# Delta-rule attention and a matmul MLP on one core: diagonal blocks of 32 solved whole from the third pair on, other norms and other unpacking in the first

## The chip, the cores and the metric

The kernel runs on one core of a Trainium2 chip. The metric is device time in microseconds (us), median of several executions. The engines are named as in the profile: PE is TensorE (PEld its weight load), DVE is VectorE, ACT is ScalarE, POOL is GpSimd, SP issues most of the DMAs.

## The reference, cut to what matters

```python
q, k, v: (4, 8, 768, 48)        beta: (4, 8, 768)
k_n = k / (norm(k) + 1e-06)
state = 0                                            # (4, 8, 48, 48)
for t in range(768):
    y[t]  = q[t] @ state
    v_old = k_n[t] @ state
    state = state + beta[t] * outer(k_n[t], v[t] - v_old)
x = y, heads side by side                            # (3072, 384)
h = x @ w_in                                         # w_in (384, 2048)
g = where(h >= 1, h, where(h <= -1, 0, (h + 1) ** 2 / 4))
return g @ w_out                                     # w_out (2048, 384)
```

The recurrence is computed in chunks of 64 steps. Within a chunk the corrected values U solve a unit lower triangular system of 64 by 64 per batch and head, built from the gram matrix of the keys, its diagonal (the squared norms) and beta; so each chunk needs the inverse of such a matrix, 32 of them at a time.

## The kernel before, in words

**Chunks and pairs.** There are 12 chunks g of 64 steps. Two chunks make a pair G, six pairs in all. For a chunk, `gram` (L138) forms K K^T and the masked K Q^T of all 32 heads, in four pieces; K K^T goes to `GG` by ACT (L147), K Q^T goes by two masked DVE multiplications (L151) into the tile `W`, which held the loaded keys and queries. The blocks of 32 on the diagonal are then transposed by DVE into "lanes" (`lanes`, L188 to L217): each of the 128 partitions holds one 32 by 32 block of the pair, so 128 small triangular systems are solved side by side along the free axis.

**The solve.** `solve` (L219) inverts the two diagonal blocks of 16 of each lane with 15 steps of two DVE instructions: a product of a column with a row (L225) and a subtraction (L227), each over 30 to 128 elements. `unlanes` (L230) scales by beta over the squared norm and transposes back (L237, L239). TensorE then joins blocks of 16 to blocks of 32 in `merge16_a` and `merge16_b` (L244, L256: 64 matmuls of 32 by 32 with 16 columns per chunk and step; each is two instructions in the trace), and blocks of 32 to 64 in `merge32_a` and `merge32_b` (L270, L286). With the inverse at hand a chunk goes through `chain_r` (V minus what the state predicts), `chain_u` (U), `chain_y` (the outputs y, which become the MLP's input tile `XB`; six small DMAs on SP per chunk, L353, shift rows) and `chain_d` (the state's update), L301 to L376.

**Norms of V.** `scale_v` (L168) scales V by the norms of its keys, which it works out again from the keys in token order: squares on ACT (L173), a reduction (L176) and five small operations (L161 to L165) on DVE.

**The MLP.** A pair gives 512 tokens. Its MLP is a loop over 16 slices of 128 hidden units, called items here: `up` (L469, nine matmuls with 512 columns), three ACT passes (L579 twice, L597) and a DVE maximum (L605), a rounding to fp32r on ACT (L574) and the remainder on DVE (L575), then `down` (L484, twelve matmuls with 384 columns). `down` of an item is issued two items later; `up` has two buffers, so it waits for the maximum of two items before. During the MLP of pair G the next pair, G+1, is prepared: `plan` (L503) writes by hand at which half item each TensorE block (`pe`) and each piece of DVE and ACT work (`fill`) is put between the MLP's instructions. The MLP of the first pair is cut differently: the first eight items only for its first chunk, eight for both, eight for the second chunk, 24 in all.

**Weights.** The MLP weights arrive as raw 64-bit words and are unpacked into two fp32r parts once (`weight`, L117: one ACT multiplication L122, DVE operations L124, L126, L128, an ACT rounding L132, a DVE subtraction L134, all over 768 elements). `unpack` (L395) hands these out in small steps, some in the opening and the rest in the first pair's items.

**The opening.** Before the first item the first two chunks are loaded and prepared with nothing to hide behind: grams, lanes, solve, merges, then chains, written out one after the other (L418 to L445). `stage` (L413) runs TensorE blocks, then evicts their results, then runs some fill.

## Time and profile before

| what | value |
|---|---|
| time, median of 3 runs | 724.34 us (724.22 to 724.47) |
| the profiled execution's own time | 723.49 us |
| its span, first to last instruction | 721.8 us |
| busy: PE, DVE, ACT, POOL | 650.7, 427.3, 402.1, 31.5 us |
| mean granted TensorE clock | 0.937 of full |
| first `up` of the first pair begins | 75.75 us |
| first `up` of the second pair's MLP begins | 233.69 us |

The profile is of one execution; times in it are counted from its first instruction. A row of a "windows" answer gives, for a stretch from A to B us, its length, the busy time of PE, PEld, DVE, ACT and POOL with their instruction counts, the granted clock, the DMA share and the GB/s moved. A timeline row gives start, length, engine, line, operation, output and inputs, and in brackets the idle time of the engine before it and what ended it; "issue" there is time in which the profile shows nothing that the engine waits for. A row of the groups gives the count, then busy us and mean ns of one.

### The profile page before, as it was taken

How to read it: one execution, taken by the hardware profiler on the slowest of the kernel's cores; microseconds unless marked ns; L12 is line 12 of the kernel's file. 1: busy time of each engine (PE TensorE's matmuls, PEld its weight loads, DVE VectorE, ACT ScalarE, POOL GpSimd, SP SyncE). 2: the span in 40 equal slices, each digit the busy share in tenths (PEclk: the TensorE clock that was granted, in tenths of full speed). 3: DMA queues.
4: the chain of work that ended last, by engine and by line, in shares of the span. 5: the costliest groups of instructions: out<-in, count | busy, mean ns of one | idle time of the engine just before them, and what ended most of it. 6: DMA issues, size and time to landing. Idle time of an engine off the chain costs nothing.

```text
span 721.8 us, 23444 instructions
## 1 busy us (share of the span) xinstructions
PE 650.7 (90%) x10436; PEld 570.0 (79%) x10436; DVE 427.3 (59%) x926; ACT 402.1 (56%) x736; POOL 31.5 (4%) x70
## 2 busy tenths in 40 slices
PE   7048768786899998999999999999999999999996
PEld 7048757565898887888888888888888888898996
DVE  4835999996346884247874347973448862433332
ACT  2017664573565563844664754657555647566663
POOL 1012000000100001000001000001000000000000
PEclk9556886897999999999999999999999999999999
DMA  9950510000017100033100033100142100001001
GB/s 244 416 233 10 157 55 1 0 1 2 11 43 185 27 1 4 3 108 107 45 2 5 5 110 102 44 4 4 29 119 68 45 4 4 13 12 45 1 1 44
DMA packets 18933, 41.72 MB, mean 58 GB/s; under 512 B 3984, under 2 KB 9488, under 8 KB 18832
## 3 DMA queue, kind: packets, MB, share of 16 engines
q1 hardware_dynamic: 17664, 38.81, 18.0%
q8 instruction: 82, 1.34, 0.8%
q10 hardware_dynamic: 912, 1.33, 0.7%
q0 software_dynamic: 256, 0.08, 0.1%
q14 instruction: 19, 0.16, 0.1%
HBM read 33.13 MB, written 4.72 MB: 52 GB/s over the span
## 4 chain that ended last, share of the span: by engine, by line
PE 73%; DVE 10%; ACT 6%; issue 2%; ACTq 0%; DVEq 0%
PE o L484 26%; PE h L469 25%; PE ch L143 4%; PE ch L319 3%; PE ch L339 3%; PE ch L363 2%; PE ch L305 2%; PE ch L248 2%; PE ch L260 2%; DVE wt L134 2%; PE ch L291 2%; PE ch L275 1%; ACT wx L122 1%; DVE s L605 1%; ACT s L579 1%
## 5 line engine op out<-in xcount | busy, mean ns | idle before, releaser
L469 PE MATMUL h<-xb,wt 128*128 128x512 f32 (+1 forms) x936 | 230.9, 391 | 7.9 <-DVE s L605 7.1
L484 PE MATMUL o<-wt,ghi 128*128 128x384 f32 x768 | 206.7, 350 | 0.5 <-issue 0.5
L469 PEld LDWEIGHTS h<-xb,wt 128*128 128x128 f32 x936 | 165.2, 192 | 45.1 <-DVE s L605 9.5
L605 DVE TENSOR_TENSOR s<-h,s 128x512 f32<-128x512 f32 (+1 forms) x104 | 67.2, 646 | 139.4 <-ACT s L597 139.2
L484 PEld LDWEIGHTS o<-wt,ghi 128*128 128x128 f32 x768 | 139.6, 192 | 9.2 <-issue 2.5
L484 PE MATMUL o<-wt,glo 128*128 128x384 f32 x384 | 132.0, 344 | 1.3 <-DVE glo L575 1.3
L579 ACT ACTIVATE s<-h,half 128x512 f32<-128x512 f32 (+1 forms) x104 | 68.1, 655 | 93.3 <-PE h L469 93.1
L575 DVE TENSOR_TENSOR glo<-s,ghi 128x512 fp32r<-128x512 f32 (+1 forms) x104 | 67.1, 645 | 46.5 <-ACT ghi L574 45.6
L574 ACT CAST ghi<-s 128x512 fp32r<-128x512 f32 (+1 forms) x104 | 61.1, 587 | 56.1 <-DVE s L605 49.3
L484 PEld LDWEIGHTS o<-wt,glo 128*128 128x128 f32 x384 | 73.4, 191 | 3.2 <-DVE glo L575 2.9
L579 ACT ACTIVATE s<-s,one 128x512 f32<-128x512 f32 (+1 forms) x104 | 71.9, 692 | 2.2
L597 ACT ACTIVATE s<-s 128x512 f32<-128x512 f32 (+1 forms) x104 | 62.3, 599 | 3.3
L143 PE MATMUL ch<-W 48*64 48x128 f32 x336 | 44.5, 286 | 10.5 <-ACT s L579 5.3
L143 PEld LDWEIGHTS ch<-W 48*64 48x64 f32 x336 | 39.1, 141 | 16.2 <-issue 9.7
L151 DVE TENSOR_TENSOR W<-ch,mask 64x256 f32<-64x256 f32 x84 | 35.5, 422 | 25.2 <-ACT GG L147 24.0
L248 PE MATMUL ch<-XT,GG 32*32 32x16 f32 x1536 | 17.9, 188 | 33.6 <-DVE XT L237 21.2
L248 PEld LDWEIGHTS ch<-XT,GG 32*32 32x32 f32 x1536 | 16.4, 118 | 37.8 <-issue 29.1
L144 PE MATMUL ch<-W 48*64 48x128 f32 x336 | 44.4, 286 | 0.0
L144 PEld LDWEIGHTS ch<-W 48*64 48x64 f32 x336 | 39.1, 141 | 0.0
L122 ACT ACTIVATE wx<-wt 128x768 f32<-128x768 f32 x16 | 14.8, 922 | 29.4 <-DVE wt L134 29.4
L147 ACT COPY GG<-ch 128x256 f32<-128x256 f32 x42 | 15.2, 372 | 27.9 <-PE ch L144 27.9
L374 DVE TENSOR_TENSOR SU<-ch,SU 48x384 f32<-48x384 f32 x40 | 22.2, 555 | 9.2 <-PE ch L363 8.5
(113 smaller groups left out, 732.0 us busy)
## 6 DMA issues: line engine op xcount, KB each, us to landing
wt<-in_w_dram SPq DMA_DIRECT2D x16, 768.0 KB, 14.8
KV<-in_kv_dram SPq DMA_DIRECT2D x24, 384.0 KB, 4.6
W<-in_kqb_dram SPq DMA_DIRECT2D x44, 128.0 KB, 3.4
W<-in_kqa_dram SPq DMA_DIRECT2D x22, 192.0 KB, 3.7
...
W<-in_kqa_dram ACTq DMA_DIRECT2D x2, 192.0 KB, 6.2
```

Of the source, the lines that this page charges most:

```text
L143: nc.tensor.matmul(gp[0:C, p], w_[C:C + D, 0, u, :], w_[C:C + D, 0:2, u, :], start=True, stop=True)
L144: nc.tensor.matmul(gp[C:P, p], w_[0:D, 0, u, :], w_[0:D, 0:3:2, u, :], start=True, stop=True)
L151: nc.vector.tensor_tensor(out=w_[r:r + C, s, us[0]:us[0] + NP], in0=gp[r:r + C, :, 1, :], in1=mask[r:r + C, None, :].broadcast_to([C, NP, ...
L248: nc.tensor.matmul(y[r:r + 32, u], GG[r:r + 32, g, u, 32:64], XT[r:r + 32, g, u, 48:64], start=True, stop=True)
L374: nc.vector.tensor_tensor(out=dst, in0=d_ps[ft:ft + D], in1=dst, op=ALU.add)
L469: nc.tensor.matmul(h[:, cols(bs)], WT[f][:, 0, x, k * P:(k + 1) * P], XB[G][:, y, k, cols(bs)], start=(n == 0), stop=(n == 8))
L484: nc.tensor.matmul(oacc[G, k], (ghi, glo)[x][:, k * P:(k + 1) * P], WT[f][:, 1, y, :], start=(new and n == 0), stop=(left[G, b] == 0 and n ...
L574: nc.scalar.copy(out=ghi[:, c], in_=s[:, c])
L575: nc.vector.tensor_tensor(out=glo[:, c], in0=s[:, c], in1=ghi[:, c], op=ALU.subtract)
L579: nc.scalar.activation(out=out, in_=in_, func=AF.Relu, bias=bias, scale=scale)
L597: nc.scalar.activation(out=s[:, c], in_=s[:, c], func=AF.Square)
L605: nc.vector.tensor_tensor(out=s[:, c], in0=h[:, c], in1=s[:, c], op=ALU.max)
```

## The change

- **From the third pair on** (G of 2 and more) the lanes' blocks of 32 are solved whole: `solve_whole` does 30 steps of two DVE instructions, in place in `A`, over 30 to 240 elements. One scaling over 1024 elements (before: two over 256) and a POOL `affine_select` and `memset` prepare `A`; `unlanes_whole` scales, transposes to `XT` and from there to `GG`. `merge16_a` and `merge16_b` are not issued for these pairs. The steps are spread over items 2.5 to 9.5 of the MLP, `merge32` moves to item 10.5, the chains and the loads move by one item, the second chunk's `chain_d` by three, the grams of the next pair's first chunk by half an item; those of its second chunk stay where they were.
- **V's norms** come from the lanes (one DVE transpose `N`) in all pairs; the squares, reductions and their small operations go.
- **First two pairs** (chunks 0 to 3): K Q^T leaves PSUM by two ACT copies and is masked by two POOL `affine_select` instructions, not by DVE. In the opening those of the second chunk are put off until after the first part of `lanes`.
- **Opening**: all loads on SP, two of the three loads of a `W` tile joined, two weights loaded ahead of K and V; 20 matmuls of 512 columns on zeros (`hold`) between the grams and the merges; `stage` evicts after its fill; in `merge32_a` the copies of `XT` go to DVE; more unpacking here (26 steps of a finer `unpack`, with four buffers, against 7 of the coarser one).
- **First pair's MLP**: four unpacking steps per item (before: two, each of two or three operations); lanes, solve, merges and chains begin earlier, the latter by three items.
- **Last store**: seven of its eight DMAs on SP (before: four).

The diff, cut:

```diff
-            q.dma_start(out=x[0:C, 0], in_=kqb[g, i][:, 0])
-            q.dma_start(out=x[0:C, 2], in_=kqb[g, i][:, 2])
+            q.dma_start(out=x[0:C, 0:3:2], in_=kqb[g, i][:, 0:3:2])
...
-    load_w(1, nc.scalar)
+    load_w(1)
...
+    weight_loads(0, 2)
     load_kv(0)
     load_kv(1)
-    weight_loads(0, FT)
+    weight_loads(2, FT)
...
             nc.scalar.copy(out=GG[:, g % 2, i * NP:(i + 1) * NP], in_=gp[:, :, 0, :])
+            def raw():
+                for r, s in ((0, 1), (C, 2)):
+                    x = w_[r:r + C, s, us[0]:us[0] + NP]
+                    nc.scalar.copy(out=x, in_=gp[r:r + C, :, 1, :])
+                    nc.gpsimd.affine_select(out=x, in_=x, pattern=[[0, NP], [1, C]], base=0, channel_multiplier=-1,
+                                            compare_op=ALU.is_gt, fill=0.0)
+            if g < 4:
+                return raw
...
+        if G >= WHOLE:
+            nc.vector.scalar_tensor_tensor(out=A, in0=A, scalar=-1.0, in1=gm[:, :, None].broadcast_to([P, 32, 32]), op0=ALU.mult, op1=ALU.mult)
+            nc.gpsimd.affine_select(out=A, in_=A, pattern=[[-1, 32], [1, 32]], base=0, channel_multiplier=0,
+                                    compare_op=ALU.is_gt, fill=0.0)
+            nc.gpsimd.memset(A.rearrange("l c t -> l (c t)")[:, 0:1024:33], 1.0)
+            return
...
+    def solve_whole():
+        A = S["A"]
+        for j in range(1, 31):
+            n, m = j, 31 - j
+            pr = sb.tile([P, 240], F32, name="pr", bufs=1)[:, 0:n * m].rearrange("l (c t) -> l c t", t=m)
+            nc.vector.tensor_tensor(out=pr, in0=A[:, 0:n, j:j + 1].broadcast_to([P, n, m]),
+                                    in1=A[:, j:j + 1, j + 1:32].broadcast_to([P, n, m]), op=ALU.mult)
+            nc.vector.tensor_tensor(out=A[:, 0:n, j + 1:32], in0=A[:, 0:n, j + 1:32], in1=pr, op=ALU.add)
+            yield
+    def unlanes_whole():
+        A, gm = S["A"], S["gm"]
+        nc.vector.tensor_tensor(out=A, in0=A, in1=gm[:, None, :].broadcast_to([P, 32, 32]), op=ALU.mult)
+        yield
+        nc.vector.transpose(out=XT[:, :, :, 32:64].rearrange("p g u t -> p t (g u)"), in_=A.rearrange("l c t -> l t c"))
+        yield
+        for g in range(2):
+            nc.vector.transpose(out=GG[:, g, :, 32:64], in_=XT[:, g, :, 32:64])
             yield
...
     def stage(pieces, *fill):
-        finish(products(*pieces))
+        evicts = products(*pieces)
         for gen, m in fill:
             run(gen, m)
+        finish(evicts)
...
+    def hold(n, m):
+        for _ in range(n):
+            nc.tensor.matmul(idle[:, 0:m], SF[:, 0:P], SF[:, 0:m], start=True, stop=True)
+    hold(KEEP, 512)
...
+            so, un = solve_whole(), unlanes_whole()
...
+            for j in range(1, 31):
+                at(fill, G, 2.5 + H / 2, (so, 1))
+                cost += j * (31 - j) + 150
+                H = int(cost / 9461 * 14)
+            for j in range(4):
+                at(fill, G, 9.5 + j // 2 / 2, (un, 1))
+            T = 1
...
+                for j, f in enumerate((merge32_a, merge32_b)):
+                    for g in range(2):
+                        at(pe, G, 10.5 + j + g / 2, lambda f=f, g=g: f(g))
...
-                at(pe, G, T + 14, *both(chain_d, b))
+                late = 0 if G == 0 else 2
+                at(pe, G, T + 14 + late, *both(chain_d, b))
                 at(fill, G, T + 14, (load_w, b + 2))
-                grams(G, T + 14.5, a + 2)
-                grams(G, T + 15.5, b + 2)
+                grams(G, T + 14 + (G == 0) / 2, a + 2)
+                grams(G, T + 14.5 + (G == 0), b + 2)
```

Where the instructions stand, at the three places that the prediction uses. First DVE in the opening, between its start and the norms; `W` are the loaded keys and queries, `ch`, `h` and `o` PSUM tiles of the grams. Before:

```order
L113 MEMSET XT 128x2048
L151 TENSOR_TENSOR W<-ch,mask 64x256 x4
L151 TENSOR_TENSOR W<-h,mask 64x256 x4
L151 TENSOR_TENSOR W<-o_204,mask 64x256 x2
L151 TENSOR_TENSOR W<-o_216,mask 64x256 x2
L151 TENSOR_TENSOR W<-o_228,mask 64x256 x2
L151 TENSOR_TENSOR W<-o_240,mask 64x256 x2
L199 COPY GG<-GG 32x16x32 x4
L201 STREAM_TRANSPOSE A<-GG 128x1024
```

and now:

```order
L115 MEMSET XT 128x2048
L202 COPY GG<-GG 32x16x32 x4
L204 STREAM_TRANSPOSE A<-GG 128x1024
L207 COPY N_281<-A 128x32
L173 TENSOR_SCALAR r_284<-y_283 128x32
```

The sixteen masks are gone from ahead of the copies into lane order. Second, PE in the opening, from the end of the grams to the first chain; `SU` is the state tile, still zero. Before:

```order
L144 MATMUL o_240<-W 64x128
L248 MATMUL ch<-XT,GG 32x16 x128
L260 MATMUL h<-A_396,XT 32x16 x128
L275 MATMUL o_620<-XT,GG 32x32 x32
L291 MATMUL o_661<-GG 32x32 x32
L275 MATMUL o_706<-XT,GG 32x32 x32
L319 MATMUL o_748<-KV,XT 64x48 x16
```

and now:

```order
L147 MATMUL o_247<-W 64x128
L471 MATMUL ch<-SU 128x512 x20
L281 MATMUL ch<-XT,GG 32x16 x64
L281 MATMUL h<-XT,GG 32x16 x64
L293 MATMUL h<-A_437,XT 32x16 x64
L293 MATMUL o_580<-A_437,XT 32x16 x64
L308 MATMUL o_652<-XT,GG 32x32 x32
L308 MATMUL o_696<-XT,GG 32x32 x32
L324 MATMUL o_737<-GG 32x32 x32
L324 MATMUL ch<-GG 32x32 x32
L352 MATMUL ch<-KV,XT 64x48 x16
```

The twenty `hold` matmuls stand ahead of the first merge, and both `merge32_a` blocks now stand ahead of `merge32_b`. Third, DVE in the MLP of the second pair, in one item in the middle of the solve for the third pair (`s`, `h`, `glo` are the MLP's tiles, `pr` a product, `X` and `A` the lanes' blocks). Before:

```order
L605 TENSOR_TENSOR s<-h,s 128x512
L225 TENSOR_TENSOR pr<-X,A_4530 128x110
L227 TENSOR_TENSOR X<-X,pr 128x2x5x11
L225 TENSOR_TENSOR pr<-X,A_4530 128x120
L227 TENSOR_TENSOR X<-X,pr 128x2x6x10
L575 TENSOR_TENSOR glo<-s,ghi 128x512
L225 TENSOR_TENSOR pr<-X,A_4530 128x126
L227 TENSOR_TENSOR X<-X,pr 128x2x7x9
L225 TENSOR_TENSOR pr<-X,A_4530 128x128
L227 TENSOR_TENSOR X<-X,pr 128x2x8x8
```

and now, an item in the middle of the longer solve:

```order
L671 TENSOR_TENSOR s<-h,s 128x512
L247 TENSOR_TENSOR pr<-A 128x220
L249 TENSOR_TENSOR A<-A,pr 128x11x20
L247 TENSOR_TENSOR pr<-A 128x228
L249 TENSOR_TENSOR A<-A,pr 128x12x19
L640 TENSOR_TENSOR glo<-s,ghi 128x512
L247 TENSOR_TENSOR pr<-A 128x234
L249 TENSOR_TENSOR A<-A,pr 128x13x18
L247 TENSOR_TENSOR pr<-A 128x238
L249 TENSOR_TENSOR A<-A,pr 128x14x17
```

As many instructions per item as before, each over about twice the elements, and for seven items in place of four.

More of the change, by code (lines that the diff above doesn't have):

```diff
@@ L168, in scale_v @@
     def scale_v(g):
[L170 to L171 removed]
         for i in range(NT):
[L173 to L183 removed]
+            v, u = KV[g, i][:, 1], g % 2 * NU + i * NV
+            nc.vector.tensor_tensor(out=v, in0=v, in1=S["N"][:, u:u + NV, None].broadcast_to([P, NV, D]), op=ALU.mult)
+            yield
     S = {}
@@ L205, in lanes @@
         r = norms(n)
+        N = S["N"] = sb.tile([P, 32], F32, name="N3")
+        nc.vector.transpose(out=N, in_=n)
         gm = S["gm"] = sb.tile([P, 32], F32, name="gm")
@@ L268, in merge16_b, with merge32_a @@
         return evict
-    def merge32_a(g):
+    def merge32_a(g, first=False):
         y1 = ps.tile([P, NU, 32], F32, **acc())
@@ L282, in evict @@
             for r in (0, C):
-                nc.scalar.copy(out=XT[r:r + 32, g, :, 0:32], in_=XT[r:r + 32, g, :, 32:64])
+                (nc.vector.tensor_copy if first else nc.scalar.copy)(out=XT[r:r + 32, g, :, 0:32], in_=XT[r:r + 32, g, :, 32:64])
         return evict
@@ L424, in delta_rule_moe @@
+    idle = ps.tile([P, 512], F32, **acc())
+    def hold(n, m):
+        for _ in range(n):
+            nc.tensor.matmul(idle[:, 0:m], SF[:, 0:P], SF[:, 0:m], start=True, stop=True)
+    hold(KEEP, 512)
+    run(ln, 2)
+    for x in raws:
+        x()
+    run(ln)
     run(solve())
     run(unlanes())
-    one_ = lambda f, g: [lambda: f(g)]
-    stage(one_(merge16_a, 0), (sv[0], 1))
-    stage(one_(merge16_a, 1), (sv[0], 2))
-    stage(one_(merge16_b, 0), (wu, 1))
-    stage(one_(merge16_b, 1), (sv[0], 9), (sv[1], 1))
@@ L431, in delta_rule_moe @@
-    stage(one_(merge32_a, 0), (wu, 1))
-    stage(one_(merge32_b, 0), (sv[1], 2))
-    stage(one_(merge32_a, 1), (wu, 1))
-    stage(both(chain_u, 0), (sv[1], 9))
-    stage(one_(merge32_b, 1))
-    stage(both(chain_y, 0), (wu, 1))
+    one_ = lambda f, *a: [lambda: f(*a)]
+    stage(one_(merge16_a, 0), (wu, 2))
+    stage(one_(merge16_a, 1), (wu, 2))
+    stage(one_(merge16_b, 0), (sv[0], 2), (wu, 1))
+    stage(one_(merge16_b, 1), (wu, 3))
+    stage(one_(merge32_a, 0, True), (wu, 2))
+    stage(one_(merge32_a, 1, True), (wu, 2))
@@ L437, in delta_rule_moe @@
+    stage(one_(merge32_b, 0), (wu, 2))
+    stage(one_(merge32_b, 1), (sv[1], 2))
+    stage(both(chain_u, 0), (wu, 3))
+    stage(both(chain_y, 0), (wu, 3))
     load_w(2)
@@ L442, in delta_rule_moe @@
             nc.gpsimd.dma_start(out=beta_sb[r + 16 * x:r + 16 * x + 16, 1:NS, :], in_=beta[q:64:4, 2 + x:ntot:2, :])
-    stage(both(chain_r, 1), (wu, 1))
-    stage(both(chain_u, 1), (wu, 1))
+    stage(both(chain_r, 1), (wu, 2))
+    stage(both(chain_u, 1), (wu, 3))
     spare.clear()
@@ L497, in at, with grams @@
         where.setdefault(2 * first[G] + int(round(2 * t)), []).extend(x)
-    def grams(G, t, g):
+    def grams(G, t, g, dt=0.5):
         for j in range(2):
-            at(pe, G, t + j / 2, *[lambda i=2 * j + x: gram(g, i) for x in range(2)])
+            at(pe, G, t + j * dt, *[lambda i=2 * j + x: gram(g, i) for x in range(2)])
     def plan(G):
@@ L526, in plan @@
-            T = 8
+            grams(G, 4, b)
+            at(fill, G, 4, (ln, 1))
+            at(fill, G, 5, (ln, 1))
+            at(fill, G, 5.5, (ln, 1))
+            at(fill, G, 6, (ln, 9))
+            for j in range(8):
+                at(fill, G, 6.5 + j / 2, (so, 2))
+            at(fill, G, 9, (va, 1))
+            at(fill, G, 9.5, (va, 1))
+            at(fill, G, 10.5, (un, 1))
+            at(fill, G, 11, (un, 9))
+            at(fill, G, 13, (vb, 1))
+            at(fill, G, 14, (vb, 1))
@@ L535, in plan @@
-            for j in range(8):
-                at(fill, G, 2.5 + j / 2, (so, 2))
-            at(fill, G, 6, (un, 1))
-            at(fill, G, 6.5, (un, 9))
-            T = 0
-        if G < NS - 1:
-            for j, f in enumerate((merge16_a, merge16_b, merge32_a, merge32_b)):
-                for g in range(2):
-                    at(pe, G, T + 7 + j + g / 2, lambda f=f, g=g: f(g))
+            at(fill, G, 1.5, (ln, 9))
+            cost, H = 0, 0
+            for j in range(1, 31):
+                at(fill, G, 2.5 + H / 2, (so, 1))
+                cost += j * (31 - j) + 150
+                H = int(cost / 9461 * 14)
@@ new lines, in plan @@
+            for j in range(4):
+                at(fill, G, 9.5 + j // 2 / 2, (un, 1))
+            T = 1
+        if G < NS - 1:
+            if G == 0:
+                for j, f in enumerate((merge16_a, merge16_b, merge32_a, merge32_b)):
+                    for g in range(2):
+                        at(pe, G, T + 7 + j + g / 2, lambda f=f, g=g: f(g))
+            else:
+                for j, f in enumerate((merge32_a, merge32_b)):
+                    for g in range(2):
+                        at(pe, G, 10.5 + j + g / 2, lambda f=f, g=g: f(g))
@@ L595, in delta_rule_moe @@
         finish(evicts)
+        run(wu, 1)
         relu(s[:, c], s[:, c], one, -1.0)
```

101 lines of the change are left out of this document (46 added, 55 removed).

## Prediction

> **What bounds the kernel now.** I read the page's 40 slices (18 us each) first, then windows between the starts of items, then timelines of the opening.
>
> ```profile
> PE   7048768786899998999999999999999999999996
> PEclk9556886897999999999999999999999999999999
> ```
>
> ```profile
> 75.75:166.21 90.46, 71.95 (x569) 59.44 (x567) 83.56 (x156) 52.88 (x98) 2.10 (x5) 0.85 0.14 41
> 166.21:239.04 72.83, 63.29 (x1510) 56.58 (x1510) 37.64 (x91) 41.09 (x92) 3.22 (x8) 0.93 0.23 61
> 265.47:283.72 18.25, 16.02 (x559) 13.09 (x555) 9.32 (x19) 6.61 (x13) 1.04 (x2) 0.91 0.02 4
> 373.22:388.24 15.02, 14.45 (x559) 12.22 (x555) 9.21 (x19) 6.61 (x13) 1.04 (x2) 1.00 0.02 5
> 454.84:471.74 16.90, 16.90 (x85) 15.24 (x85) 14.63 (x46) 11.33 (x20) 0.96 (x1) 1.00 0.19 47
> 478.06:492.14 14.08, 14.04 (x559) 11.99 (x555) 9.19 (x19) 6.62 (x13) 1.07 (x2) 1.00 0.02 6
> 581.63:596.53 14.90, 14.58 (x557) 12.24 (x555) 9.19 (x19) 6.61 (x13) 1.04 (x2) 1.00 0.02 4
> ```
>
> Three stages. To 75.75 us nothing hides anything, and the clock is half for most of it. From 75.75 to 166.21 (first pair's MLP up to the transposes that end the solve) DVE is busy 83.56 of 90.46 us: it bounds. From the second pair's MLP on PE bounds: the four items from 454.84 take 16.90, PE busy all of it, 4.225 per item. There, what PE no longer does is time won, as long as DVE (14.63 of the same 16.90) does not become the bound.
>
> **Merges of 16, pairs three to six.** The four windows of two items each that hold them (18.25, 15.02, 14.08, 14.90) last 62.25 together; eight bare items are 33.80. Removed: **-28.4**, waits in them included.
>
> **DVE in those pairs.** Step prices, from the opening's solve:
>
> ```profile
> 26.12 0.19 DVE L225 TENSOR_TENSOR pr<-X,A 128x30 f32<-128x30 f32 x1
> 30.11 0.29 DVE L225 TENSOR_TENSOR pr<-X,A 128x128 f32<-128x128 f32 x1
> 34.85 0.76 DVE L235 TENSOR_TENSOR A<-X,gm 128x256 f32<-128x256 f32 x2
> ```
>
> From 30 to 128 elements an instruction grows by 0.10, so 0.16 us plus 1.0 ns per element. The old solve lasts 26.12 to 34.85 = 8.7 for 30 instructions over 2720 elements, which by that are busy 7.6: a gap of 0.04 behind each. The new one has 60 over 9920 elements (twice the sum of j(31-j)): 60 x 0.20 + 9.9 = 21.9, or 20 if the gap vanishes wherever the MLP's own instructions come between. What stands beside it:
>
> ```profile
> 427.72:435.80 8.08, 8.08 (x122) 6.92 (x118) 5.17 (x11) 4.41 (x9) 0.33 (x1) 1.00 0.18 43
> 444.20:450.63 6.43, 6.43 (x56) 5.57 (x54) 5.08 (x12) 3.58 (x7) 0.00 (x0) 1.00 0.01 3
> 444.20:478.06 33.86, 33.86 (x246) 30.22 (x244) 28.92 (x75) 20.88 (x35) 0.96 (x1) 1.00 0.10 24
> 471.74:478.06 6.32, 6.32 (x87) 5.60 (x86) 5.07 (x12) 3.49 (x6) 0.00 (x0) 1.00 0.01 3
> L605 DVE TENSOR_TENSOR s<-h,s 128x512 f32<-128x512 f32 (+1 forms) x104 | 67.2, 646 | 139.4 <-ACT s L597 139.2
> L374 DVE TENSOR_TENSOR SU<-ch,SU 48x384 f32<-48x384 f32 x40 | 22.2, 555 | 9.2 <-PE ch L363 8.5
> L151 DVE TENSOR_TENSOR W<-ch,mask 64x256 f32<-64x256 f32 x84 | 35.5, 422 | 25.2 <-ACT GG L147 24.0
> 476.81 2.25 DVE L237 STREAM_TRANSPOSE XT<-A 128x1024 f32<-128x1024 f32 x1
> ```
>
> DVE from item 0 to the transposes that merge32 waits for, by item 9.5: 28.92 of items 0 to 6; less the old steps, their two scalings of 0.76 and the transpose begun there at 476.81 (7.6 + 1.5 + 1.3); plus solve 20 to 22, four masks 1.7, chain_d 4 x 0.555 = 2.2, two scalings over 1024 elements 2.4 (by the step's price), transpose 2.2, chain_r's two subtractions some 1.1, and for three more items L605 and the remainder of the same size, 1.3 each: **52.5 to 54.5**. PE in the same stretch, to merge32_a at the end of item 10: 6.43 (item 0 with two grams), 8.08 - 6.43 = 1.65 for chain_d, 6.32 for the item with chain_r, nine others at 4.225: 52.4. A tie. DVE starts about 1 us late, since the grams end first, but an up waits only for the maximum of two items before. What lies over is a wait of PE at merge32_a: 1 to 2 us per pair, **+5** for four (0 to 16). Behind the waiting merge32 stand both chains, so it cannot be made up.
>
> POOL's select over 1024 elements sits between the scaling and the first step. Nearest row:
>
> ```profile
> L101 POOL TENSOR_SCALAR_AFFINE_SELECT mask<-mask 64x64 f32<-64x64 f32 x2 | 0.5, 232 | 0.1
> L216 POOL MEMSET A<- 128x1024 f32 x6 | 5.7, 956 | 162.5 <-DVE A L214 162.5
> ```
>
> Between 0.96 (a memset of that size) and 3.7 (0.232 for 64, scaled). I take 1.5, nearer the memset of equal size, since most of 0.232 looks fixed; it is covered by the MLP's two DVE instructions of 0.65 and a scaling of V that stand between. At 3.7 the solve starts 2 us later, +9 for four pairs; that is in the 16. [...]
>
> **Loads for the second chunk's grams.** These grams stay at items 15.5 and 16; their loads move from item 14 to 15, behind six row DMAs of chain_y, now at 14.5.
>
> ```profile
> 429.33 4.50 SPq L353 DMA_DIRECT2D xb<-X  x6
> 435.16 0.58 SPq L72 DMA_DIRECT2D W<-in_kqa_dram  x1
> W<-in_kqa_dram SPq DMA_DIRECT2D x22, 192.0 KB, 3.7
> ```
>
> The up of the item that starts at 427.72 follows chain_y directly; the row DMAs end 6.1 later, the first tile's last load is issued at 7.4 and lands at 11.1. PE now reaches the gram after up, two grams, down, two grams: 4.2 + 4 x 1.05 = 8.4. It waits 2.7, in three pairs: **+8** (3 to 9). Nothing hides it: PE is in order.
>
> **The opening.**
>
> ```profile
> L97 PE MATMUL o<-wx 128*128 128x128 f32 x28 | 6.1, 414 | 1.1 <-DVE half L104 1.1
> 7.14 0.32 PE L143 MATMUL ch<-W 48*64 48x128 f32 x1
> 10.16 1.28 ACT L108 ACT_TABLE_LOAD   x1 [10.16 <-DMA W<-in_kqa_dram]
> L147 ACT COPY GG<-ch 128x256 f32<-128x256 f32 x42 | 15.2, 372 | 27.9 <-PE ch L144 27.9
> 19.00 1.70 DVE L199 COPY GG<-GG 32x512 f32<-32x512 f32 x4
> 37.97 2.76 PE L248 MATMUL ch<-XT,GG 32*32 32x16 f32 x193 [21.22 <-DVE XT L237]
> 44.71 0.99 PE L248 MATMUL ch<-XT,GG 32*32 32x16 f32 x60 [3.97 <-issue]
> 49.45 0.42 DVE L265 TENSOR_TENSOR XT<-XT,h 128x256 f32<-128x256 f32 x1 [2.03 <-PE h L260]
> 69.70 0.28 DVE L349 TENSOR_TENSOR X<-h,X 128x128 fp32r<-128x128 f32 x1
> 75.75 0.50 PE L469 MATMUL h<-xb,wt 128*128 128x256 f32 x2
> ```
>
> The first gram starts at 7.14, but ACT only at 10.16, after its DMA issues; then the masks hold DVE until 19.00. Now ACT is free and copies as grams end, from about 7.4: twelve copies of 0.37 for the first chunk's grams and four for the second's reach 13.3 (the second chunk's loads no longer share the DMA engines with K and V). Before, DVE's four copies into lane order lasted from 19.00 to 20.70; now the first chunk's two are done by 13.3 and the second's two end 0.85 later, at 14.15, which is 6.55 earlier. The new transpose `N` takes some 0.2 of that; so all down to the merge at 37.97 moves up by about 6.4, to 31.5.
>
> The `hold` matmuls stand before that merge on PE. 28 instructions over 128 columns took 6.1 at the start, 0.22 each; 512 columns in two instructions are 1.74 at that rate, 35 for twenty, and 17 if the clock is twice as fast by then, as the first digit of its row says. From 11.6 (my estimate for the last gram on PE, one or two copies of 0.37 ahead of ACT's last ones) they end at 29, beneath the solve, and cost nothing; at the slow rate they would end at 47.
>
> The merges: in one of them PE lost 3.97 to nothing that the profile shows, while weights still loaded. Starting earlier, more of the merging lies in that time; I add 2. The first result of merge16_b came at 49.45, 11.5 after the first merge; now at 31.5 + 11.5 + 2 = 45. DVE waits for it, then has until chain_y's remainders about 18 to 19 us without a pause: five weights of 3.4 (prices below) and 2 for copies, less what of it came ahead. That is 64; the first up came 6 after the last remainder (69.70, 75.75), so now near 70.3. V's norms, gone, lay beside the merges' waits. **-5.4** (-10 to +10).
>
> **First pair's MLP.**
>
> ```profile
> L134 DVE TENSOR_TENSOR wt<-wx,wt 128x768 fp32r<-128x768 f32 x15 | 14.2, 948 | 0.0
> L128 DVE SCALAR_TENSOR_TENSOR wx<-wt,wx 128x768 int32<-128x768 int32 x14 | 13.3, 952 | 0.0
> L124 DVE TENSOR_SCALAR wx<-wx 128x768 int32<-128x768 int32 x13 | 7.8, 602 | 0.6 <-ACT wx L122 0.6
> ```
>
> A weight costs DVE 0.60 and three times about 0.95 (L126 is of L128's kind): 3.4. Some 3.6 fewer here: -12; sixteen masks x 0.42: -6.7; the solve's transposes come at item 11 instead of 14, three full items' 1.3 off: -4. That leaves 67 to 68 of 90.46; I take 70, for ACT now carries some 8 us in each of the two items with eight copies of 0.37 more. After it PE bounds: before, the 72.83 from 166.21 on held 10 of waits (72.83 - 63.29) and half-clock time (0.93); now it has three full items more in it (12.7) and some 10 less of waits and slow clock: 75.5. **-18** (-10 to -26).
>
> **Small.** A PE idle of 2 to 3 us can lower the clock, as it did in the second pair (0.91 in the first merge window): **+3** (0 to 10). At the end SP issues three DMAs more, of 0.58 each by the row above, while ACT's last copy comes sooner: **+0.5**.
>
> **Sum.** -28.4 + 5 + 8 - 5.4 - 18 + 3 + 0.5 = -35.3. The profiled execution took 723.49 (its span 721.8 and 1.7 around it): 688.2; the median lies 0.85 above it: **689**.
>
> **Rivals.**
>
> (1) *The hold keeps the clock up through merges and chains.*
>
> ```profile
> 60.00:64.00 4.00, 4.00 (x93) 3.91 (x93) 2.21 (x6) 3.83 (x8) 0.00 (x0) 0.50 0.02 4
> 68.00:72.00 4.00, 3.06 (x112) 2.81 (x109) 3.16 (x7) 3.27 (x7) 0.00 (x0) 0.97 0.06 14
> ```
>
> The clock fell in the opening's solve and stayed at 0.50 through merges and chain_u, which kept PE busy 4.00 of 4; it rose at 68. I therefore let it fall again in the merges. If it does not, the chains of the opening run at full speed, -5, and the pairs' +3 goes: 681. [...] Chance 0.17.
>
> (2) *DVE, not PE, bounds pairs three to six*: every gap kept, 3.7 us for the select, the clock falling at each wait: 16 in place of 5 and 10 in place of 3, +18: 707. Chance 0.21.
>
> (3) *The change doesn't do what it says in front*: the hold runs at the slow rate and ends at 47, where the merges would start at 31.5: the opening grows by 10 instead of shrinking by 5.4, 704; with (2) as well, 722. Against it: the clock was full when the grams ended. Chance 0.07, most of it with (2).
>
> (4) *Slower.* In-place steps with a strided column cost more than the old ones: at 0.22 us more on each of 60, DVE needs 13 more per pair, all of it waited for by PE since the two are tied: +53, 742. Slower begins at +35, 0.15 per step. The old steps read a strided column too and show no such cost at 30 or 128 elements. Chance 0.05.
>
> The forecast itself has 0.50, its own range 678 to 700. The range, 669 to 711, takes in (1) and (2), with their errors on the outer side, leaving out (4) and most of (3). Faster by more than 0.2% (1.4 us, what this measurement can tell): 0.94; within: 0.01; slower: 0.05.
>
> **What would show it.** Right: the first up near 70; the second pair's first up near 212; PE busy nearly all the time later, with waits of 1 to 2 us for the transpose to `XT` at merge32_a and near 2.7 for a `W` load at item 15.5; solve steps of 0.41 at 240 elements. Wrong: DVE above 95% busy in items 2 to 9 with PE waits at every up; a first up after 76; no wait for `W`.

## The result, and the profile after

The changed kernel takes 714.07 us (median of 4, 712.81 to 715.24) where the kernel before took 724.28: a ratio of 0.9859, 95% interval 0.9822 to 0.9896. It is faster, by 10 us and not by the 35 that were forecast; 714 lies above the range.

Its profiled execution has a span of 712.25. The 40 slices of its page, to be laid beside those of before (17.8 us each here):

```profile
PE   8848776679999899998999999999989999999996
PEclk9955988799999999999999998999998999999999
```

PE no longer rests before the merges (much of the second slice's 8 is `hold`), but the third slice, the merges, is 4, and the fifth to the ninth, the first pair's front, are 6 and 7. The windows of the changed kernel, cut at the start of the first item, of the first pair's item 11, and of the third item of each later pair (the last cut stands at the first plain item of the last pair):

```profile
0.00:76.08 76.08, 57.66 (x1284) 45.63 (x1284) 48.49 (x98) 32.45 (x64) 17.70 (x41) 0.78 0.61 216
76.08:153.01 76.93, 51.74 (x419) 43.28 (x415) 56.96 (x110) 43.89 (x90) 9.97 (x21) 0.80 0.18 48
153.01:236.42 83.41, 82.43 (x1675) 73.65 (x1676) 41.85 (x87) 50.53 (x101) 2.07 (x4) 1.00 0.20 53
236.42:340.16 103.74, 98.73 (x1233) 85.37 (x1233) 71.82 (x156) 60.54 (x107) 3.83 (x6) 1.00 0.14 35
340.16:445.50 105.34, 101.63 (x1234) 88.08 (x1234) 70.11 (x155) 58.83 (x104) 3.84 (x6) 0.97 0.18 45
445.50:551.18 105.68, 101.78 (x1233) 88.17 (x1233) 70.11 (x155) 58.82 (x104) 3.83 (x6) 0.97 0.17 45
551.18:634.33 83.15, 80.41 (x1000) 69.67 (x999) 56.42 (x128) 50.34 (x87) 3.83 (x6) 1.00 0.09 25
```

and the kernel before, cut at the same items (in the first pair the solve, the merges and the chains now stand some three items earlier, so its two rows do not part the same work; their sum does):

```profile
0.00:75.75 75.75, 41.44 (x1245) 39.37 (x1245) 43.98 (x108) 24.15 (x50) 10.54 (x25) 0.68 0.62 217
75.75:141.71 65.96, 49.68 (x418) 42.32 (x415) 60.48 (x116) 37.58 (x75) 2.10 (x5) 0.79 0.19 56
141.71:242.21 100.50, 88.73 (x1675) 76.46 (x1676) 63.39 (x136) 58.45 (x118) 3.22 (x8) 0.95 0.17 44
242.21:350.00 107.79, 105.56 (x1746) 91.27 (x1745) 64.02 (x143) 61.74 (x112) 4.18 (x9) 0.98 0.15 41
350.00:454.84 104.84, 104.17 (x1746) 90.56 (x1745) 62.44 (x143) 61.28 (x112) 4.18 (x9) 1.00 0.18 46
454.84:558.40 103.56, 103.52 (x1745) 90.22 (x1745) 62.42 (x143) 61.29 (x112) 4.22 (x9) 1.00 0.18 47
558.40:644.23 85.83, 85.51 (x1512) 74.80 (x1511) 44.89 (x105) 52.45 (x93) 3.03 (x5) 1.00 0.07 16
```

| stage | before | after | difference | forecast |
|---|---|---|---|---|
| opening, to the first item | 75.75 | 76.08 | +0.33 | -5.4 |
| from there to the second pair's third item | 166.46 | 160.34 | -6.1 | -18 |
| from there to the last pair's first plain item | 402.02 | 397.91 | -4.1 | -28.4 + 5 + 8 + 3 = -12.4 |
| the rest | 77.55 | 77.92 | +0.4 | +0.5 |

In the third row PE has some 500 instructions fewer per pair (1234 for 1746) and is busy 2 to 7 us less of each, yet the two stretches that begin in the third and in the fourth pair are longer than before, at a granted clock of 0.97. In the second row the first part, up to item 11, became 11 us longer, with DVE busy 56.96 of 76.93.

### The profile page after: what moved, and what is told of

It is laid out like the page before. It is cut to its first block, busy times and chain, and to the rows that moved or that the text cites. A ratio compares the mean times of both kernels' runs of the same rounds, so it can differ in the third digit from the quotient of the medians.

```text
span 712.2 us, 19365 instructions
## 1 busy us (share of the span) xinstructions
PE 646.0 (91%) x8428; PEld 558.4 (78%) x8428; DVE 440.7 (62%) x920; ACT 400.1 (56%) x720; POOL 45.1 (6%) x90
## 3 DMA queue, kind: packets, MB, share of 16 engines
q8 instruction: 66, 1.08, 0.6%
## 4 chain that ended last, share of the span: by engine, by line
PE 47%; DVE 33%; ACT 6%; issue 5%; DMA 4%; SPq 3%; DVEq 0%; ACTq 0%
PE h L522 15%; PE o L537 14%; DVE pr L247 5%; DVE A L249 4%; DVE s L671 4%; DVE glo L640 4%; DMA W<-in_kqa_dram 3%; PE ch L372 3%; PE ch L352 3%; SPq L386 2%; PE ch L146 2%; PE ch L324 2%; PE ch L396 2%; PE ch L308 2%; PE ch L338 2%
## 5 line engine op out<-in xcount | busy, mean ns | idle before, releaser
L522 PEld LDWEIGHTS h<-xb,wt 128*128 128x128 f32 x936 | 167.9, 194 | 52.2 <-DVE s L671 16.6
L537 PE MATMUL o<-wt,ghi 128*128 128x384 f32 x768 | 202.0, 344 | 2.4 <-ACT ghi L639 2.4
L537 PEld LDWEIGHTS o<-wt,ghi 128*128 128x128 f32 x768 | 138.1, 189 | 11.6 <-ACT ghi L639 3.0
L146 PE MATMUL ch<-W 48*64 48x128 f32 x336 | 47.8, 300 | 17.7 <-DMA W<-in_kqa_dram 7.0
L146 PEld LDWEIGHTS ch<-W 48*64 48x64 f32 x336 | 42.3, 150 | 23.4 <-issue 13.9
L147 PE MATMUL ch<-W 48*64 48x128 f32 x336 | 48.0, 300 | 0.0
L163 DVE TENSOR_TENSOR W<-ch,mask 64x256 f32<-64x256 f32 x64 | 27.0, 422 | 32.6 <-ACT GG L150 31.7
L249 DVE TENSOR_TENSOR A<-A,pr 128x30 f32<-128x30 f32 (+14 forms) x120 | 39.8, 332 | 4.4
L147 PEld LDWEIGHTS ch<-W 48*64 48x64 f32 x336 | 42.2, 150 | 0.0
L247 DVE TENSOR_TENSOR pr<-A 128x30 f32<-128x30 f32 (+14 forms) x120 | 39.3, 328 | 2.2
L218 POOL TENSOR_SCALAR_AFFINE_SELECT A<-A 128x1024 f32<-128x1024 f32 x4 | 6.4, 1593 | 370.4 <-DVE A L217 370.4
L135 ACT CAST wt<-xb 128x768 fp32r<-128x768 f32 x16 | 13.3, 832 | 28.9 <-DVE xb L131 28.9
## 6 DMA issues: line engine op xcount, KB each, us to landing
wt<-in_w_dram SPq DMA_DIRECT2D x16, 768.0 KB, 13.7
```

The source lines that it names most:

```text
L146: nc.tensor.matmul(gp[0:C, p], w_[C:C + D, 0, u, :], w_[C:C + D, 0:2, u, :], start=True, stop=True)
L147: nc.tensor.matmul(gp[C:P, p], w_[0:D, 0, u, :], w_[0:D, 0:3:2, u, :], start=True, stop=True)
L163: nc.vector.tensor_tensor(out=w_[r:r + C, s, us[0]:us[0] + NP], in0=gp[r:r + C, :, 1, :], in1=mask[r:r + C, None, :].broadcast_to([C, NP, ...
L247: nc.vector.tensor_tensor(out=pr, in0=A[:, 0:n, j:j + 1].broadcast_to([P, n, m]), in1=A[:, j:j + 1, j + 1:32].broadcast_to([P, n, m]), op= ...
L249: nc.vector.tensor_tensor(out=A[:, 0:n, j + 1:32], in0=A[:, 0:n, j + 1:32], in1=pr, op=ALU.add)
L522: nc.tensor.matmul(h[:, cols(bs)], WT[f][:, 0, x, k * P:(k + 1) * P], XB[G][:, y, k, cols(bs)], start=(n == 0), stop=(n == 8))
```

## The experiments

Numbers in brackets are the median of the experiment; all medians of before in these series lie between 723.0 and 724.2. Times of places are from the one profile of each.

**The W loads** [701.74; ratio to before 0.9679, 0.9651 to 0.9707].

```diff
-                at(fill, G, T + 14, (load_w, b + 2))
+                at(fill, G, T + 13.5, (load_w, b + 2))
```

> Loads of the second chunk's W tiles issued ahead of chain_y's six row DMAs, no other change. Theory: the waits of PE for W at item 15.5 (1.79, 2.15 and 2.32 us in pairs two to four) go, and with the two longer ones the slower clock behind them (0.86 and 0.80 of full over 22 us), which cost more than the waits: some 11 us in all, 703. Rival 1, the prediction's size: only the waits go, the clock falls anyway: 6 us, 708. Rival 2: the row DMAs, now 2.7 us later, make the first up of the next pair wait for XB, 2 to 3 us in each of three pairs: 710 to 714.

SP and PE in the changed kernel, third pair: six row DMAs, then four loads, and PE's first gram that needs them.

```profile
419.27 3.87 SPq L386 DMA_DIRECT2D xb<-X  x6
423.92 0.59 SPq L73 DMA_DIRECT2D W<-in_kqa_dram  x1
428.24 0.44 PE L146 MATMUL ch<-W 48*64 48x128 f32 x1 [2.15 <-DMA W<-in_kqa_dram]
```

Windows of the two items there, of the second pair (two rows) and of the third; the granted clock stands ahead of the last two columns.

```profile
315.70:327.80 12.10, 10.31 (x120) 8.83 (x117) 6.40 (x15) 4.97 (x11) 0.00 (x0) 1.00 0.40 93
327.80:334.20 6.40, 6.40 (x55) 5.54 (x54) 4.12 (x10) 3.58 (x7) 0.00 (x0) 1.00 0.01 3
417.70:431.80 14.10, 11.96 (x119) 10.35 (x117) 6.87 (x16) 4.97 (x11) 0.00 (x0) 0.86 0.36 80
431.80:439.60 7.80, 7.80 (x56) 6.59 (x55) 3.69 (x8) 3.58 (x7) 0.00 (x0) 0.81 0.00 0
```

and with the loads first, third pair:

```profile
414.90:425.80 10.90, 10.36 (x121) 8.85 (x117) 6.46 (x15) 4.97 (x11) 0.00 (x0) 1.00 0.50 104
425.80:432.20 6.40, 6.40 (x55) 5.51 (x54) 4.04 (x10) 3.58 (x7) 0.00 (x0) 1.00 0.00 0
```

The second pair's wait of 1.79 cost only itself; behind the third pair's of 2.15 the clock was 0.86 and 0.81, and the two items lasted 21.9 where they last 17.3 with the loads first. The theory's size (11) holds: 12.3 in all, against the 6 of the waits alone. Of it, 10.6 lie from the second pair's third item on (397.9 us became 387.3), the rest in the first pair, whose loads this edit moves as well. The late row DMAs made nothing wait.

**The hold** [715.20; ratio 0.9882, 0.9838 to 0.9926].

```diff
-KEEP = 20
+KEEP = 0
```

> Without the twenty hold matmuls. The prediction's: they cost nothing and keep no clock, since the clock is 0.50 in the merges anyway (granted clock 0.78 from 32 to 38 us, 0.50 from 38 on): 714, within 0.5. Rival: the clock falls earlier without them and the first merges run at half speed: the 126 matmuls from 35.14 that took 1.76 take about the same, since they wait for instructions, but the stalls come earlier: 713 to 717. Second rival: the stalls in the merges come from the hold (PE fetches behind it): the time falls by 2 to 4.

No difference that its interval can tell. The first item starts at 74.77, 1.3 earlier. The clock is 0.50 from 20 to 64 us without the hold; with it 1.00 from 20 to 32, 0.78 to 38 and 0.50 from there to 68: with it the clock stays up while PE has nothing else, and the merges run at half all the same. PE's four waits in the merges are 3.58, 4.17, 1.82 and 1.03 us without the hold (3.87, 4.17, 1.82 and 1.29 with it), so the waits do not come from the hold; that PE waits for instructions in them, as both rivals assume, no run here shows.

**The opening's stalls** [8 late: 720.12, 0.994 (0.9912 to 0.9968); 10 late, on the loads-first kernel: 695.54, 0.9608 (0.9581 to 0.9635)].

```diff
-    weight_loads(2, FT)
+    weight_loads(2, 8)
...
     load_w(2)
+    weight_loads(8, FT)
```

> Weights 8 to 15 are loaded after chain_y of the first chunk, not before the merges. Theory: the four stalls of PE in the opening's merges in which the profile shows nothing it waits for (3.87, 4.17, 1.82, 1.29 us) come from the weights' loads, which keep the DMA share at 1.02 until 45 us; without them the sum of 11.2 falls to about 4, the first result of merge16_b comes near 42 in place of 48.9, the first up near 71, and the time falls by 4 to 5, to 709. Rival: they do not depend on the loads (the last two came after the loads had ended) but on how fast the small matmuls use up instructions; then they stay near 11, the first up stays near 76 and the time near 714.

PE in the opening's merges, changed kernel (start, length, ..., and in brackets the idle time ahead):

```profile
35.14 1.76 PE L281 MATMUL ch<-XT,GG 32*32 32x16 f32 x126 [2.77 <-DVE XT L270]
41.15 1.52 PE L281 MATMUL h<-XT,GG 32*32 32x16 f32 x100 [3.87 <-issue]
47.22 1.52 PE L293 MATMUL h<-A,XT 32*32 32x16 f32 x99 [4.17 <-issue]
50.94 1.42 PE L293 MATMUL o<-A,XT 32*32 32x16 f32 x91 [1.82 <-issue]
54.40 1.81 PE L308 MATMUL o<-XT,GG 32*32 32x32 f32 x60 [1.29 <-issue]
```

and with weights 8 to 15 loaded later:

```profile
33.75 1.22 PE L281 MATMUL ch<-XT,GG 32*32 32x16 f32 x126 [2.77 <-DVE XT L270]
37.12 1.52 PE L281 MATMUL h<-XT,GG 32*32 32x16 f32 x100 [1.86 <-issue]
40.72 1.52 PE L293 MATMUL h<-A,XT 32*32 32x16 f32 x99 [1.70 <-issue]
44.17 1.42 PE L293 MATMUL o<-A,XT 32*32 32x16 f32 x91 [1.55 <-issue]
47.63 2.82 PE L308 MATMUL o<-XT,GG 32*32 32x32 f32 x98 [1.29 <-issue]
78.45 0.89 ACT L125 ACTIVATE xb<-wt 128x768 f32<-128x768 f32 x1 [11.47 <-DMA wt<-in_w_dram]
```

The four stalls ("issue") fell from 11.2 in all to 6.4, the first merge starts 1.4 earlier, and the first item came at 69.14, 6.9 earlier: 4.8 of the stalls go with the weights' loads, the larger part does not. But the whole kernel got slower than the changed one, which neither theory had. In the last row ACT's first step on weight 8, which stands ahead of the evictions, waits 11.47 us for its load, with all engines behind it (from 72 to 76 us PE, DVE and ACT are busy for 0.00); by the second pair's third item the kernel is 2.3 behind the changed one. The other 4 of the 6 us came later, where the waits for W were 2.98, 2.21 and 2.66. So the second try loads ten weights early, on the kernel with the W loads first:

```diff
-    weight_loads(2, FT)
+    weight_loads(2, 10)
...
     load_w(2)
+    weight_loads(10, FT)
```

> On the kernel with the loads ahead of the row DMAs (701.7): weights 10 to 15 are loaded after chain_y of the first chunk. The late load of weights 8 to 15 had brought the first up from 76.1 to 69.8 and then held ACT 11.5 us for weight 8; weight 10 is touched two items later. Theory: the first up comes at 70 to 71 and nothing waits for a weight; the first pair is then bounded as before, so some 5 us go: 697. Rival: what the opening wins is given back in the first pair, since its weights are fewer by the time of the first up: 700 to 702.

First item at 69.65, no wait for a weight, 6.2 us less: what the opening wins is kept. The stalls stand between runs of 128 matmuls (of two tiles together) with as many weight loads, and the changed kernel's page gives for the queue that it calls "instruction" 1.08 MB in 66 packets, 16 KB each:

```profile
q8 instruction: 66, 1.08, 0.6%
```

and in the kernel before:

```profile
q8 instruction: 82, 1.34, 0.8%
```

The two pages count 16,856 of PE's matmuls and weight loads as changed and 20,872 before, 255 for each of these packets in both, where a run between two stalls has 256. Such a run, at 16 columns, lasts about 2 us (1.9 from 41.15), and between two runs PE stood idle for 1.3 to 4.2 us. That the stalls are waits for these packets is the author's inference from the spacing; no run here tests it.

**The whole solve by itself** [717.91; ratio 0.9917, 0.9890 to 0.9944]. Blocks of 16 and the old plan in every pair, all else as changed:

```diff
-WHOLE = 2
+WHOLE = 6
...
-            T = 1
+            for j in range(8):
+                at(fill, G, 2.5 + j / 2, (so, 2))
+            at(fill, G, 6, (un, 1))
+            at(fill, G, 6.5, (un, 9))
+            T = 0
```

> The changed kernel with the blocks of 16, merge16 and the old plan of items in every pair (chain_d, loads and grams where they stood before); the opening, the first pair, the norms and the last store as changed. The prediction's terms for this part, merges -28.4, DVE +5 and W +8, make it worth 15.4: then this kernel takes 729. What the two traces show from item 26 to item 88 (408.0 us before, 397.9 after, 2 of that from plain items of 4.19 in place of 4.23) makes it worth some 4 to 8 with the W waits eating the rest: 718 to 722. Rival: the W waits and the slower clock behind them eat all of it: 714.

This is near the 718 to 722 that the traces had led to expect, and not the 729 of the prediction's terms. As changed, the whole solve is worth 3.8 us; with its W waits taken away (701.74) it is worth 16.2. In the profiles the stretch from the second pair's third item to the last pair's first plain one takes 400.73 here, 397.91 as changed, 387.29 with the loads first.

**DVE beside POOL's select** [689.76; ratio 0.9540, 0.9524 to 0.9556]. The kernel with the loads first and ten weights early (695.54), leaving out masks that the result needs:

```diff
-                    nc.gpsimd.affine_select(out=x, in_=x, pattern=[[0, NP], [1, C]], base=0, channel_multiplier=-1,
-                                            compare_op=ALU.is_gt, fill=0.0)
...
-            nc.gpsimd.affine_select(out=A, in_=A, pattern=[[-1, 32], [1, 32]], base=0, channel_multiplier=0,
-                                    compare_op=ALU.is_gt, fill=0.0)
```

> On the same kernel (695.5), leaving out POOL's affine_selects: the masks of chunks 0 to 3 and that of the lanes' blocks are not applied. Theory 1: in the opening DVE's small steps (0.39 to 0.44 beside the selects) fall back to 0.19 and its two scalings from 1.22 to 0.76, so the solve starts 1 to 1.5 earlier. Theory 2: in pairs three to six the select (1.59) was 0.6 to 1.4 of each item pair at the solve's start and 0.9 at merge32; without it these go: 2 to 2.5 in each of four pairs, 8 to 10 us: 684 to 687. Rival: DVE's own sum bounds there and only the memset's wait goes: 692 to 694.

DVE in the opening, changed kernel, beside POOL's selects, and the same lines without them:

```profile
21.02 0.43 DVE L213 TENSOR_TENSOR gm<-r,beta_sb 128x32 f32<-128x32 f32 x1
21.49 0.44 DVE L214 TENSOR_TENSOR gm<-gm,r 128x32 f32<-128x32 f32 x1
21.96 1.22 DVE L225 TENSOR_TENSOR A<-A,gm 128x256 f32<-128x256 f32 x2
```

```profile
20.17 0.19 DVE L211 TENSOR_TENSOR gm<-r,beta_sb 128x32 f32<-128x32 f32 x1
20.40 0.19 DVE L212 TENSOR_TENSOR gm<-gm,r 128x32 f32<-128x32 f32 x1
20.62 0.76 DVE L221 TENSOR_TENSOR A<-A,gm 128x256 f32<-128x256 f32 x2
```

and in the third pair of the changed kernel, POOL's select and DVE's scaling of V, which took 0.55 at other times:

```profile
346.53 1.59 POOL L218 TENSOR_SCALAR_AFFINE_SELECT A<-A 128x1024 f32<-128x1024 f32 x1 [97.87 <-DVE A L217]
346.92 1.60 DVE L184 TENSOR_TENSOR KV<-KV,N 128x384 f32<-128x384 f32 x1
351.71 0.55 DVE L184 TENSOR_TENSOR KV<-KV,N 128x384 f32<-128x384 f32 x1
```

The scaling that began 0.39 after the select ended 0.40 after it, and took 1.60 for 0.55; in the opening DVE's steps over 32 elements took 0.43 to 0.44 beside the selects and 0.19 without them. What the two engines share there no run shows. Theory 1 holds for the opening's solve: the first merge comes 1.2 earlier (33.34 for 34.57), though the first item only 0.5. The selects cost about 1.1 in each of four pairs (from item 2 to item 10 of the third pair 36.31 for 37.44); the wait at merge32 (0.88 as changed, 0.97 without) stayed, so theory 2 had half its size. The two scales of time differ here: the medians are 5.8 apart, the profiles 3.4.

**The first pair.** Six runs asked what bounds items 0 to 11. First DVE's masks put back for chunks 2 and 3 [718.18; ratio 0.9906, 0.9876 to 0.9936]:

```diff
-            if g < 4:
+            if g < 2:
```

> The second pair's grams (chunks 2 and 3) are masked by DVE again, not copied by ACT and masked by POOL. Theory: in items 2 to 6 of the first pair ACT and DVE wait for each other in turn (ACT's rounding of a weight for DVE, DVE's glo for ACT's ghi behind the copies), so 8 copies of 0.38 per gram item are on the path and 4 masks of 0.42 less so: the waits of PE for W at these grams (0.99, 0.94, 5.08 us) shrink, item 7 starts 3 to 5 us earlier, 709 to 711. Rival, the prediction's: DVE's sum bounds the first pair, sixteen masks of 0.42 more are 6.7 us: 718 to 721.

To item 11 it takes 76.70 instead of 76.93, with DVE busy 63.09 instead of 56.96. Six us more of DVE work cost nothing there, so DVE's sum does not bound; nor do ACT's copies cost more than the masks. The median is what the rival named (718), but not by its mechanism: the 4 us came later, where the waits for W were 3.02, 2.50 and 3.20. What DVE waits for, around item 5 of the changed kernel (`xb` and `wt` are the weight that is being unpacked):

```profile
114.03 0.42 DVE L671 TENSOR_TENSOR s<-h,s 128x256 f32<-128x256 f32 x1 [0.36 <-ACT s L663]
115.35 0.96 DVE L131 SCALAR_TENSOR_TENSOR xb<-wt,xb 128x768 int32<-128x768 int32 x1
116.35 0.83 ACT L135 CAST wt<-xb 128x768 fp32r<-128x768 f32 x1 [1.55 <-DVE xb L131]
117.20 0.65 ACT L150 COPY GG<-ch 128x256 f32<-128x256 f32 x2
117.73 1.55 ACT L155 COPY W<-ch 64x256 f32<-64x256 f32 x4
119.31 0.41 ACT L639 CAST ghi<-s 128x256 fp32r<-128x256 f32 x1
119.74 0.54 DVE L640 TENSOR_TENSOR glo<-s,ghi 128x256 fp32r<-128x256 f32 x1 [3.43 <-ACT ghi L639]
```

The maximum that ghi reads ends at 114.45, but on ACT ghi stands behind the rounding, which waits for DVE, and behind six copies; it starts at 119.31, and DVE sits idle for 3.43.

Then, on the loads-first kernel, two other orders: two unpacking steps fewer in the opening, which shifts the four steps of each item [708.17; 0.9779, 0.9751 to 0.9807], and ghi ahead of left-over evictions [701.62; 0.9694, 0.9668 to 0.9721].

```diff
-    stage(both(chain_u, 1), (wu, 3))
+    stage(both(chain_u, 1), (wu, 1))
```

> On the kernel with the loads first (701.7): two unpacking steps fewer in the opening, so that the four steps of an item stand shifted by two: ACT's rounding of a weight comes behind the evictions and ahead of the second relu, not last before the next ghi. Theory: items 2 to 6 are bounded by a ring of ACT and DVE (maximum, two DVE steps of a weight, ACT's rounding, ghi, relu, eviction copies, squares, maximum); with the shift the copies lie beside the DVE steps, DVE's idle time there shrinks and item 7 starts 4 to 7 us earlier: 695 to 698. Rival: the sum of DVE's work bounds, as the prediction had it: within 1 of 701.7.

```diff
+        if last and item[0] == 0:
+            rest(*last)
         finish(late)
         if last:
-            rest(*last)
+            if item[0] > 0:
+                rest(*last)
```

> On the kernel with the loads first (701.7): in the first pair ghi and glo of an item are issued ahead of the evictions left over from its second half, so ghi no longer stands behind two copies to GG and four to W on ACT. Theory (the ring of ACT and DVE): two such lots of 2.2 us leave the ring, 2 to 4 us go: 698 to 700. Rival: PE's grams wait for these evictions, and they come later now: no gain or a loss of 1.

The shift lost 6 where 4 to 7 were to be won: to item 7 it took 45.33 (44.95 in the kernel it was built on, 46.79 as changed), but from there to item 11 36.16 (30.16; 30.14), with DVE busy 27.02 in it (27.66 as changed). As much work on DVE in another order is 6 us longer. The theory of a ring gains, my picture of its best order falls: ACT's rounding, ahead of the second relu, waits 3.0 to 5.1 for DVE steps that now stand behind the solve's (1.3 to 3.7 as changed). The second order won 1.5 to item 11 and gave it back at items 12 and 16 by waits of PE: no gain, as its rival said. Kept to nine items, without the hold, on the kernel with the late weights [693.83; 0.9602, 0.9587 to 0.9616] it kept 1.7:

```diff
-KEEP = 20
+KEEP = 0
...
+        if last and n < 9:
+            rest(*last)
         finish(late)
         if last:
-            rest(*last)
+            if n > 8:
+                rest(*last)
```

> On the kernel with loads first and weights 10 to 15 late (695.5): ghi and glo ahead of the left-over evictions, as in the run before, but only in the first nine items, and no hold. The same order over all items of the first pair had brought item 11 from 151.1 to 148.1 (1.5 of it before the first item) and given it back by waits of PE in items 12 and 16 (1.62 and 1.12). Theory: 1.5 to 2.5 of it stays, hold costs nothing or 1: 692 to 694. Rival: nothing stays, since what bounds items 7 to 11 is another thing: 695.

Then, again on the kernel with the late weights (695.54), ACT's rounding of weights 6 to 15 was given to POOL [692.00; 0.9570, 0.9549 to 0.9591], and chunk 3's W loads put ahead of the first pair's row DMAs as well [687.67; 0.9507, 0.9479 to 0.9535].

```diff
-        nc.scalar.copy(out=hi, in_=x)
+        (nc.scalar.copy if f < 6 else nc.gpsimd.tensor_copy)(out=hi, in_=x)
```

> On the same kernel (695.5): POOL, not ACT, rounds weights 6 to 15 to fp32r. Theory, the ring: ACT's rounding, which waits for DVE's last step of a weight and holds the next ghi behind it, is off ACT; items 2 to 10 take 6 to 10 less: 686 to 690. Rival: POOL's pass over 768 elements and DVE's two-input steps get in each other's way (in the opening, beside POOL's selects, DVE's 32-element steps took 0.43 where they took 0.19 before): DVE loses 0.5 to 1 per weight and the gain goes, 695 to 700.

```diff
-            at(fill, G, 1, (load_w, 3))
+            at(fill, G, 0, (load_w, 3))
```

> On the kernel with POOL's rounding (692.0): chunk 3's W loads issued ahead of chain_y's six row DMAs in the first pair too, where these rows took 12.15 us on SP and PE then waited 4.65 us for W at the fourth chunk's grams. Theory, the ring: with ACT's rounding away, nothing but this load holds items 2 to 6, so most of the 4.65 goes and item 7 starts some 4 earlier: 688. Rival: DVE's sum bounds by now (DVE busy over 96% in items 8 to 10), what PE gains in item 4 it loses in items 5 to 8: 691 to 692.

POOL's rounding alone won 3.5, less than its theory said. PE then waited for a load behind row DMAs, which took 12.15 us there:

```profile
80.23 12.15 SPq L386 DMA_DIRECT2D xb<-A  x6
```

```profile
98.34 0.41 PE L146 MATMUL ch<-W 48*64 48x128 f32 x1 [4.65 <-DMA W<-in_kqa_dram]
```

and with that wait gone, items 0 to 11 of the last kernel, to be laid beside the second row of the changed kernel's windows:

```profile
68.79:137.51 68.72, 47.04 (x420) 39.62 (x416) 61.80 (x110) 36.17 (x81) 22.41 (x31) 0.85 0.38 122
```

68.72 for 76.93, DVE busy 90% of it for 74%. From 75.68 in the kernel with the late weights, the rounding took away 3.2 (72.50) and the load 3.8. So ACT's rounding is shown to be a link; the ring's other links are read from the rows. DVE is near its bound now, partly because its 110 instructions there last 61.80 and lasted 56.96 before POOL's rounding: the rival of that run holds too (step L127 takes 0.87 on average for 0.58).

**All together** [685.61; ratio to before 0.9476, 0.9446 to 0.9506], with V's scaling of the first chunk two items later, ghi ahead of left-over evictions in the first nine items, and no hold:

```diff
-                at(fill, G, 2 + j, (va, 1))
+                at(fill, G, 4 + j, (va, 1))
```

> All together: loads first in every pair, weights 10 to 15 late, POOL's rounding, ghi ahead of left-over evictions in the first nine items, no hold, and V's scaling of the first chunk from items 2 and 3 to 4 and 5, so that it no longer stands beside POOL's select (0.55 took 1.60 there). Theory: the last is worth 1.0 in each of four pairs as leaving out the selects was, the order of ghi 1 to 1.5, W of chunk 3 another 3 to 4: 682 to 685. Rival: V's scaling only moves within a DVE that is full there (4.0 to 4.15 of items of 4.2), so 686 to 689.

The fastest of all. The rival had the later pairs right: the third pair's stretch from item 2 to item 10 takes 37.03 (37.44 as changed), not 36.3: items 3 and 4 shrink (4.82 and 4.99 became 4.56 and 4.19), but item 6, where part of the scaling now stands, grows from 4.18 to 4.88. It is 2.1 under the kernel with chunk 3's loads first by the medians, 0.2 by the profiles.

## Why the prediction was wrong, step by step

The forecast was 25.8 too low by the spans: 5.7 in the opening, 11.9 in the first pair, 8.3 in pairs two to five.

- **Merges of 16, -28.4: stands.** In the kernel with the blocks of 16 the four windows of two items with merges are 27.3 longer than bare items. Against it, with the loads first, the stretch of pairs two to five is 13.4 shorter (400.73, 387.29): the merges, less what DVE took back (next item), 0.5 of waiting at each of three grams, and smaller waits.
- **DVE a tie, +5 (0 to 16): right in kind, too small.** The solve's 60 steps are busy 79.1 for four pairs, 19.8 each, where 20 to 22 was said; POOL's select took 1.59, where 1.5 was said. (DVE's terms as listed add up to 52.0 to 54.0, not 52.5 to 54.5; the tie stays.) But in the third to fifth pair items 3, 4, 5 and 8 are 1.7 over 4.19 together and merge32 waits 0.9: 2.6 each. In the second pair it is some 4, of which 1.6 stands in the kernel with the blocks of 16 too. That is 10 to 11 in all. Some 4 us of it, by the run without the selects, was missing from the working, which let V's scaling cover part of the select; beside the select it took 1.60, and 0.55 at other times.
- **W loads, +8 (3 to 9), with +3 (0 to 10) for the clock: 12.3.** Place and order were right. The waits were 6.3 in all, where 8 was said, and 1.6 of them stay with the loads first; the slower clock behind the two longer ones cost 6.0, where 3 was said; the rest lies in the first pair.
- **The opening, -5.4: +0.3.** The first merge came at 35.14, not 31.5: the second chunk's last W landed at 13.0, so that the copies into lane order ended at 16.31 and not at 14.15, and DVE's small steps from the norms to the solve took 1.4 longer beside POOL's selects (4.95 from L207 on, 3.55 without the selects). From there to merge16_b's first result it took 13.7 (48.88), as the 11.5 + 2 said, though the stalls that the 2 stood for come at every 128 matmuls, and some of them could be had. From that result to the first item it took 27.2, not 25.3; this 1.9 was not looked into.
- **The step that failed: the first pair, -18.** "That leaves 67 to 68 of 90.46; I take 70": it took DVE's work off the length of the stage, as if DVE's sum set it. To the point that 166.21 marks before (the end of the first of the transposes, 159.99 here) it took 83.9 after the first item, with DVE idle for a quarter of the time; what follows, up to the second pair's second item, took 73.3, where 75.5 was said. Before, DVE was busy 92% of the stage, and taking work from it was read as taking time; but four unpacking steps per item and the copies on ACT closed a ring: DVE's last step of a weight ahead of its rounding, ACT's rounding, ACT's ghi and copies behind that, the relu and square, DVE's maximum, and DVE's next step behind the maximum. The runs show that the stage costs the same whether DVE masks or not (76.70, 76.93), 6.4 more in another order (81.49, 75.10), and 7.0 less once the rounding is off ACT and W comes in time (75.68, 68.72). Then the first transposes end 75.6 after the first item, which is nearer to the 70 and not there.
- **The hold, nothing: right.** So was it to give the rival that it keeps the clock up in the merges little (0.50 from 38 to 64 us with the hold and without).
- **The signs to look for.** The first item after 76 was named as a sign of a wrong forecast, and came true (76.08); the second pair's first item, looked for near 212, came at 230; the waits at merge32 (1 to 2 said, 0.9 seen) and for W (2.7 said, 1.8 to 2.3 seen) came as named.

None of the rivals was this case. The one nearest in time (DVE bounds the later pairs, 707) has a part of the mechanism and not the larger ones.
